# Moving a second attention into the segment loop of a tuned kernel, giving an output projection four column tiles of 128 outputs, and reordering the segment

## The chip, the cores and the metric

The kernel runs on one core of one Trainium2 chip. The metric is the device time of one execution, in microseconds (us). Before the change it was 1159.68 us, the median of three runs (1159.42 to 1160.88). TensorE is called PE below, ScalarE ACT, VectorE DVE, GpSimd POOL; PEld is PE's weight load, which runs beside the matmuls (in before PE is busy for 1012.0 us and PEld for 559.7, in a span of 1153.9).

## The reference, cut to what matters

Two attentions work on the same 2048 x 512 input, and a gate per token mixes their results.

```
# A: 64 segments of 32 tokens, 32 heads of 128, 8 memory tokens carried on
mem = mem0
for s in range(64):
    h = concat([mem, x[32*s : 32*s+32]])           # 40 tokens
    q, k, v = h @ Wq, h @ Wk, h @ Wv               # each 512 -> 32 heads x 128
    p = softmax(mask(q @ k^T * scale))
    o = einsum(p @ v, Wo)                          # 4096 -> 512
    mem, out[s] = o[:8], o[8:]                     # the next segment needs mem

# B: 4 blocks of 512 tokens, 32 heads of 16; block by block causal softmax attention
#    plus a linear memory M, z of the earlier blocks; then @ wo
result = g * A + (1 - g) * B                       # g: sigmoid gate per token
```

A is one long chain: segment s+1 cannot be projected before segment s has left Wo. B has no such chain and can fill gaps. The kernel cuts B into 160 **steps**: the scores and the exp of one step, then its product with V. Ten steps make one of 16 **jobs** (4 heads on each half of the partitions; the operands of a job are brought from DRAM, to which the projections of B were stored).

## The kernel before

A static order of units is emitted for every segment; each engine is given its instructions in that order, with semaphores where one engine needs another's result.

```
A_ORDER = """
    K1 K0 Q0 Q1 Fc TK0 TQ0 TK1 Ff bP TQ1 bT Fc S0 bS V0 M0 S1 N0 V1 M1 N1 PV0 Fc E0a E0b PV1 W0 E1a E1b W1 Fc bP bP bS
    WT bS Ff bT""".split()
```

K, Q, V are the projections of head groups 0 and 1; TK, TQ the transposes; S the scores with their exp (ACT); M the softmax sums with Ln and Exp on ACT; N the normalization (DVE); PV the product with V; E its evictions; W the two halves of Wo; WT the transposition of Wo's result into the next segment's input. bS, bP, bT are pieces of B. Fc and Ff are **fill units**: projections of the last 8 tokens of the four segments of a group, which are not on the chain (Fc), and their transposes and the end of a finished group (Ff).

Wo before, per segment: 32 matmuls of 512 columns. Each of four column tiles (32 token rows) holds a partial sum over 8 of the 32 heads; the partial sums are added afterwards by a product with a selector `selL`, for which the float32 result is split into a high and a low bfloat16 part.

```
for i in range(4):
    for j in range(4):                                   # column tile j: heads 16b+4j+i
        h = 16 * b + 4 * j + i
        ins = pe.matmul(pb[bk][SEG * j:SEG * (j + 1), :], OT_sb[:, h, 0:SEG], Wo_sb[:, h, :], ...)
...                                                      # after b == 1:
evac("act", aW_sb[:, 0, cs], pb[bk][:, cs], ...)                                       # hi, twice
P.op("dve", ... d.tensor_tensor(aW_sb[:, 1, cs], pb[bk][:, cs], aW_sb[:, 0, cs], ALU.subtract))  # lo, twice
...                                                      # w_t: 8 products with selL, adding hi and lo
ins = pe.matmul(pb[bk][:, SEG * c:SEG * (c + 1)], aW_sb[:, k, 128 * c:128 * (c + 1)], selL[:, :], ...)
```

Ahead of the loop stand B's projections, mixed with 40 of the 160 B steps. For those steps the job's buffers are double (`KTa`/`KTb`, `QTa`/`QTb` and so on); the other 120 steps run in the loop with one set of buffers. [... loads, constants, gates and the scheduler are cut ...]

## Time and profile before

| what | value |
|---|---|
| time, median of 3 | 1159.68 us |
| stage 1, up to the first segment | 0 to 174 us, granted clock 0.81 |
| segment loop, 64 segments | 174 to 1146 us, 15.2 us a segment, granted clock 1.00 |
| end | 8 us |

The first two lines below are from the profile's page of the kernel before; each digit stands for a fortieth of the span (29 us). "PE" is its busy share in tenths, "PEclk" the clock that PE was granted, in tenths of full speed (9 means 0.9 or more).

```profile
PE   4667769999999999999999999999999998988886
PEclk8798779999999999999999999999999998999999
```

The windows view of before gives the same by stages: length, busy time of each engine with its instruction count, the mean granted clock, the share in which DMA engines were busy, and GB/s.

```profile
core 0: us, PE busy (x) PEld busy (x) DVE busy (x) ACT busy (x) POOL busy (x), PEclk, DMA share, GB/s
0.00:174.00 174.00, 113.19 (x987) 57.68 (x1005) 57.49 (x111) 69.85 (x95) 86.26 (x178) 0.81 0.56 186
174.00:1146.00 972.00, 896.27 (x23349) 500.86 (x23356) 432.18 (x1116) 620.70 (x1329) 162.42 (x395) 1.00 0.06 16
```

PE is idle for a third of stage 1 (busy for 113.19 of 174 us), and its clock is low there (0.81). In the loop PE is busy for 896 of 972 us at full clock: it is the limit. The little that it waits is in the view of PE's waits of before (line and result that waited, releaser, us in total, times, longest):

```profile
PE ps L1102 <- DVE Pn_sb L1092: 25.4, 62, 0.9
PE ps L1160 <- ACT LN_sb L312: 14.8, 31, 0.9
PE ps L726 <- DMA QTa<-scr_qTd: 13.1, 5, 11.8
...
PE ps L1160 <- ACT VL L312: 4.8, 11, 0.9
PE ps L1160 <- DVE aW_sb L1149: 4.7, 4, 1.4
```

L1102 is PV, waiting for the normalized probabilities `Pn_sb`: 0.4 us in nearly every segment. L1160 is the product with the selector. It waits 24.3 us in the whole run (14.8 + 4.8 + 4.7), 0.4 us a segment. The timeline of PE in before (start, length, line, result and operands, count; in brackets the idle time just ahead and what ended it) shows the stretch from the first scores to the second PV:

```profile
560.33 1.05 PE L876 MATMUL ps<-Wv_sb,hT 128*32 128x512 bf16 x16
561.21 0.27 PE L1077 MATMUL ps<-P_sb,onesb 128*32 128x160 bf16 x8
...
561.40 0.27 PE L1050 MATMUL ps<-QT_sb,KT_sb 128*32 128x40 bf16 x16
561.50 0.29 PE L1054 MATMUL ps<-QT_sb,KTL 128*32 128x16 bf16 x16
561.62 1.06 PE L876 MATMUL ps<-Wv_sb,hT 128*32 128x512 bf16 x16
562.50 0.28 PE L1077 MATMUL ps<-P_sb,onesb 128*32 128x160 bf16 x8
562.72 0.27 PE L1102 MATMUL ps<-Pn_sb,V_sb 32*128 32x40 bf16 x16
...
563.01 0.62 PE L876 MATMUL ps<-Wq_sb,xL 128*32 128x512 bf16 x8
564.01 0.28 PE L1102 MATMUL ps<-Pn_sb,V_sb 32*128 32x40 bf16 x16 [0.39 <-DVE Pn_sb L1092]
```

Both V projections (0.87 us each, from start to start) and one fill unit (`Wq_sb,xL`) lie inside the stretch and cover nearly all of ACT's and DVE's chain. (The 16 score matmuls of 40 columns at 561.40 take 0.10 us to the next start, 6.5 ns each.) I call it the **thin stretch**, since this is where PE has least to do of its own.

### The profile page before, as it was taken

What the parts mean: (1) busy time and instruction counts of PE and PEld (TensorE: products, weight loads), DVE (VectorE), ACT (ScalarE), POOL (GpSimd) and SP (SyncE); (2) the same over time, 40 slices, a digit from 0 to 9 for tenths busy, and PEclk for the clock granted to TensorE, in tenths of its full rate; (3) what the DMA queues carried; (4) which work ended last, traced back from release to release, by engine and by line L of the source; (5) the groups of instructions that cost most, each with busy time, mean ns of one, the idle gap of its engine ahead of it and who ended that gap; (6) DMA issues with size and microseconds to landing.
All of it is one profiled execution on the core that took longest, in us unless ns stands there. A gap on an engine that the chain in (4) does not pass through costs nothing. (4 is left out here: it accounts for less than half of the span.)

```text
span 1153.9 us, 54295 instructions
## 1 busy us (share of the span) xinstructions
PE 1012.0 (88%) x24359; PEld 559.7 (49%) x24389; DVE 491.1 (43%) x1229; ACT 692.1 (60%) x1427; POOL 248.7 (22%) x573
## 2 busy tenths in 40 slices
PE   4667769999999999999999999999999998988886
PEld 2333325555555555555555555555555554544443
DVE  2333334444444444444444444444444443434333
ACT  2455336666666666666666666666666664555554
POOL 6554431211212121212122111212122110000000
PEclk8798779999999999999999999999999998999999
DMA  9486310010101001010100001010100000000000
GB/s 309 141 278 226 105 62 3 3 32 4 36 5 27 13 11 29 8 32 8 27 12 23 12 9 31 8 33 7 28 12 23 18 3 21 3 12 4 12 12 7
DMA packets 50943, 47.59 MB, mean 41 GB/s; under 512 B 23184, under 2 KB 49176, under 8 KB 49176
## 3 DMA queue, kind: packets, MB, share of 16 engines
q1 hardware_dynamic: 50712, 44.13, 12.3%
q8 instruction: 192, 3.15, 1.1%
q14 instruction: 39, 0.32, 0.1%
HBM read 31.50 MB, written 12.61 MB: 38 GB/s over the span
## 5 line engine op out<-in xcount | busy, mean ns | idle before, releaser
L742 POOL TENSOR_SCALAR_AFFINE_SELECT PTa<-PTa 128x256 bf16<-128x256 bf16 (+1 forms) x205 | 90.1, 440 | 419.1 <-ACT PTa L734 387.6
L734 ACT ACTIVATE PTa<-ps 128x1024 bf16<-128x1024 f32 x147 | 150.4, 1024 | 42.2 <-PE ps L726 40.6
L876 PE MATMUL ps<-Wv_sb,hT 128*32 128x512 bf16 x2048 | 134.9, 381 | 2.0 <-ACT QT_sb L312 1.3
L312 ACT ACTIVATE QN_sb<-ps 128x512 bf16<-128x512 f32 x128 | 76.4, 597 | 89.5 <-PE ps L876 89.5
L876 PE MATMUL ps<-Wk_sb,hT 128*32 128x512 bf16 x2048 | 123.3, 383 | 3.7 <-DVE hT L1166 2.6
L1139 PE MATMUL ps<-Wo_sb,OT_sb 128*32 128x512 bf16 x2048 | 126.2, 381 | 0.1
L876 PE MATMUL ps<-Wq_sb,hT 128*32 128x512 bf16 x2048 | 121.6, 379 | 0.0
L314 DVE CAST V_sb<-ps 128x512 bf16<-128x512 f32 x128 | 88.5, 691 | 73.1 <-PE ps L1077 40.5
L1149 DVE TENSOR_TENSOR aW_sb<-ps,aW_sb 128x256 bf16<-128x256 f32 x128 | 48.4, 420 | 128.1 <-ACT aW_sb L312 126.1
L312 ACT ACTIVATE aW_sb<-ps 128x256 bf16<-128x256 f32 x128 | 42.2, 381 | 92.5 <-PE ps L1139 92.5
L1191 POOL COPY OTL<-OT_sb 128x256 bf16<-128x256 bf16 x64 | 25.4, 397 | 319.4 <-DVE OT_sb L314 319.4
L312 ACT ACTIVATE OT_sb<-ps 128x320 bf16<-128x320 f32 x192 | 75.7, 428 | 24.9 <-PE ps L1111 24.9
L312 ACT ACTIVATE QT_sb<-ps 128x512 bf16<-128x512 bf16 x128 | 77.0, 601 | 22.3 <-PE ps L885 22.3
L876 PEld LDWEIGHTS ps<-Wq_sb,hT 128*32 128x32 bf16 x2048 | 54.8, 97 | 55.8
L726 PE MATMUL ps<-QTa,KTa 32*128 32x512 bf16 (+1 forms) x448 | 55.6, 305 | 24.4 <-DMA QTa<-scr_qTd 13.1
L314 DVE CAST KN_sb<-ps 128x512 bf16<-128x512 f32 x64 | 44.2, 690 | 75.6 <-PE ps L876 75.6
L876 PEld LDWEIGHTS ps<-Wk_sb,hT 128*32 128x32 bf16 x2048 | 49.2, 97 | 53.5 <-DVE hT L1166 5.1
L314 DVE COPY KT_sb<-ps 128x512 bf16<-128x512 bf16 x64 | 27.2, 425 | 111.0 <-PE ps L885 111.0
L1139 PEld LDWEIGHTS ps<-Wo_sb,OT_sb 128*32 128x32 bf16 x2048 | 46.6, 95 | 49.9 <-ACT OT_sb L312 20.7
L876 PEld LDWEIGHTS ps<-Wv_sb,hT 128*32 128x32 bf16 x2048 | 47.2, 95 | 38.1 <-issue 6.7
L312 ACT ACTIVATE KN_sb<-ps 128x512 bf16<-128x512 f32 x64 | 38.2, 597 | 43.2 <-PE ps L876 43.0
L1081 ACT ACTIVATE R_sb<-ps 128x160 f32<-128x160 f32 x128 | 38.8, 303 | 33.7 <-PE ps L1077 33.3
(146 smaller groups left out, 1802.5 us busy)
## 6 DMA issues: line engine op xcount, KB each, us to landing
Wk_sb<-in_A_Wk_dram SPq DMA_DIRECT2D x4, 1024.0 KB, 7.9
Wq_sb<-in_A_Wq_dram SPq DMA_DIRECT2D x4, 1024.0 KB, 5.6
Wv_sb<-in_A_Wv_dram SPq DMA_DIRECT2D x4, 1024.0 KB, 6.4
Wo_sb<-in_A_Wo_dram SPq DMA_DIRECT2D x4, 1024.0 KB, 6.3
scr_vd<-V SPq DMA_DIRECT2D x16, 136.0 KB, 2.2
Wo_sb<-in_A_x_dram SPq DMA_DIRECT2D x4, 512.0 KB, 8.2
scr_kTd<-stgk SPq DMA_DIRECT2D x16, 128.0 KB, 3.9
scr_qTd<-stgq SPq DMA_DIRECT2D x16, 128.0 KB, 4.6
```

Of the source, the lines that this page charges most:

```text
L312: P.op("act", lambda a: a.activation(dst, src, ACT.Copy), reads=[v.rbank[k] for k in bks], writes=dres, name=name)
L314: P.op("dve", lambda d: d.tensor_copy(dst, src), reads=[v.rbank[k] for k in bks], writes=dres, name=name)
L726: ins = pe.matmul(v.pb[bks[x]][:, o:o + w], KT[e][r, 128 * kc:128 * (kc + 1)], QT[r, q0:q0 + w], start=True, stop=True, tile_position=(r.s ...
L734: P.op("act", lambda a: a.activation(pt[:, :, :], v.ps[:, bks[0]:bks[1] + 1, :], ACT.Exp, scale=v.SCALE_B), reads=[v.rbank[b] for b in bks ...
L742: P.op("gp", lambda g, mv=mv: g.affine_select(mv, mv, [[0, mv.shape[1]], [1, 128]], ALU.is_ge, 0.0, base=0, channel_multiplier=-1), reads= ...
L876: ins = pe.matmul(pb[bk][SEG * j:SEG * (j + 1), :], lhs(c), w_sb[:, c, n0:n0 + 512], start=(c == 0), stop=(c == C - 1))
L1081: P.op("act", lambda a: a.activation(R_sb[:, b, :], pb[bk][:, 224:384], ACT.Ln), reads=[rbank[bk]], writes=[Rs("R%d" % b)], name="ln%d_%d" ...
L1139: ins = pe.matmul(pb[bk][SEG * j:SEG * (j + 1), :], OT_sb[:, h, 0:SEG], Wo_sb[:, h, :], start=(b == 0 and i == 0), stop=(b == 1 and i == 3))
L1149: P.op("dve", lambda d, cs=cs: d.tensor_tensor(aW_sb[:, 1, cs], pb[bk][:, cs], aW_sb[:, 0, cs], ALU.subtract), reads=[rbank[bk], Rs("aWh%d ...
L1191: P.op("gp", lambda gq: gq.tensor_copy(OTL[par][:, :, 8 * r:8 * r + 8], OT_sb[:, :, SEG:L]), reads=[Rs("OT%d_%d" % (c, hf)) for c in range ...
```

## The change

The intent has three parts. (1) No B step ahead of the loop any more: stage 1 holds only projections, and all 160 steps become fill in the loop; the results of A and B pass through DRAM, and the buffers of the B jobs become single. (2) Wo gets column tiles of 128 outputs each: 128 matmuls of 128 columns instead of 32 of 512. Each tile sums over all heads, so no partial sums, no split and no selector remain; one transpose makes the next input. (3) A new order of the segment. The diff, cut to its core (cuts marked by dots):

```diff
 A_ORDER = """
-    K1 K0 Q0 Q1 Fc TK0 TQ0 TK1 Ff bP TQ1 bT Fc S0 bS V0 M0 S1 N0 V1 M1 N1 PV0 Fc E0a E0b PV1 W0 E1a E1b W1 Fc bP bP bS
-    WT bS Ff bT""".split()
+    Q0 K0 K1 Q1 TK0 bP TQ0 TK1 TQ1 V0 S0 bS M0 Ff bT S1 N0 V1 M1 N1 PV0 E0b bP E0a PV1 E1a E1b bP bS Ff bT Fc Fc W0 W1
+    bS WT Ff""".split()
 ...
-                for i in range(4):
+                for h in range(16 * b, 16 * b + 16):
                     for j in range(4):
-                        h = 16 * b + 4 * j + i
-                        ins = pe.matmul(pb[bk][SEG * j:SEG * (j + 1), :], OT_sb[:, h, 0:SEG], Wo_sb[:, h, :],
-                                        start=(b == 0 and i == 0), stop=(b == 1 and i == 3))
+                        ins = pe.matmul(pb[bk][SEG * j:SEG * (j + 1), 0:128], OT_sb[:, h, 0:SEG], Wo_sb[:, h, 128 * j:128 * (j + 1)],
+                                        start=(h == 0), stop=(h == H - 1))
 ...
-                for k in range(2):
-                    evac("act", aW_sb[:, 0, cs], ...)          # hi
-                for k in range(2):
-                    P.op("dve", ... ALU.subtract ...)           # lo
+                evac("dve", aW_sb[:, :], pb[bk][:, 0:128], [bk], [Rs("aW")], "aW%d" % s)
 ...
-            for k2 in range(2): ... 8 products with selL ...
+            P.op("pe", lambda pe: pe.transpose(pb16[bk][:, 0:128], aW_sb[:, :], ident[:, :]), ...)
 ...
-    for n in range(n_pre):                                      # 40 B steps among the projections
-        bat.scores() ... bat.pv()
+    for n in range(len(pieces)): ... pieces[n]()                # projections alone
 ...
-    n_b0, nseg_b = bat.n, DEV.get("nseg_b", 51)
+    n_b0, nseg_b = bat.n, DEV.get("nseg_b", 57)
```

The fill units of projections also become whole (16 matmuls instead of two halves of 8), and four of the copies out of PSUM (where PE's results go, `ps` in the views; the kernel uses it in banks) change between ACT and DVE (`A_ENG`). In the new order V0 stands ahead of S0; no Fc stands between PV0 and PV1.

## The prediction

It was made from the code, the diff and the profile of before alone.

> **What bounds the kernel now.** The windows view shows three stages. (1) 0 to 174 us, until the first segment's K projection: projections of B mixed with 40 of the 160 B steps. PE is 64% busy and its mean granted clock 0.6 to 0.9 [...]. Waits between engines bound it. (2) 174 to 1146 us: 64 segments of 15.1 us, PE 93 to 95% busy at clock 1.00. From starts in the timeline I count 14.1 us of issued work and 0.8 us of idle a segment (0.37 before the second PV, on DVE Pn_sb; 0.25 before the selL product). (3) 8 us of end.
>
> **Removed.** Per segment the hi/lo split (ACT 2 x 381 ns, DVE 2 x 420 ns, in series) and 8 selL matmuls (0.46 us of PE). From the end of Wo to the next K takes 2.3 us with nothing between (last segment, timeline); a DVE copy of 128 columns (about 0.29 us, from casts of 490 and 690 ns for 320 and 512), a transpose and the hT cast (190 ns) should take 1.1. Stage 1 loses 40 B steps (about 0.7 us of PE, 1.02 of ACT each), their loads and chains.
>
> **Added, moved.** Wo becomes 128 matmuls of 128 columns: the same streaming, 4 times the instructions. The 40-column score matmuls issue every 6.5 ns, so issue is no limit: 1.8 to 2.0 us against 1.8. The loop gets 2.8 B steps a segment for 2.35: +0.3 us of PE. The new order puts V0 ahead of the scores and the fill behind E1. From the first scores to the second PV takes 4.4 us (timeline), set by ACT (exp, the 1.02 us B exp, Ln, Exp, exp, Ln, Exp). PE fills all but 0.4 us of it now; the new order leaves it about 2.9 us of work there. So I expect about 1 us of new idle, which eats the gain at the segment's end: 15.2 to 15.7 us with B steps, 14.2 in the last seven. All jobs now have single buffers, with scores slots 4 to 6 us apart, against 6.8 us from the first K load to Q's landing: waits of 1 to 3 us in about 10 of 16 job changes (now 1.3 us in most of the loop), some on V; 10 to 45 us in all.
>
> **Sum (estimates from those durations).** Stage 1: 65 us of PE, or 24 MB at the first slice's 300 GB/s, 80 us; with left projections and start-up 95 (-78). Loop: 57 x 15.4 + 7 x 14.2 + 25 of DMA waits = 1003 (+31). End: aT through DRAM, two groups in series: 18 (+9). Total 1116 us; range 1075 to 1148. Faster by over 2%: 0.70; within 2%: 0.27; slower: 0.03.
>
> **Signs.** Right: first segment near 95 us, higher clock before it; the aW split gone; PE idle before the sums and the second PV grows; PE waits on DMAs of QTj and Vj in the loop; PE busy under 93% in the loop; the last 18 us thin. Wrong: segments of 14.5 us or less without new idle (then about 1060), or Wo over 2.2 us.
>
> **What would make it wrong.** Stage 1 stalling on stores queued behind 1 MB weight loads; ACT's order misjudged; Wo's weight loads not hidden; clock drops from new idle.

## The result, and the profile after

The kernel after took 1241.14 us, the median of four runs (1229.38 to 1242.89), against 1159.55 us for before in the same rounds (1157.56 to 1160.88). The ratio is 1.068, with a 95% interval of 1.062 to 1.075: **slower by 6.8%**, where 1116 us and a gain had been predicted. Ratios here and below are the mean time of one kernel's fast runs over that of the other's of the same rounds, so they are not quite the ratios of the medians quoted.

The same two lines of the page, for after (a digit is 31 us):

```profile
PE   8978888888888898878898988798879888888884
PEclk9989999899989899889899989899999989999997
```

The windows of after, by its own stages:

```profile
0.00:90.00 90.00, 74.08 (x525) 37.14 (x529) 48.84 (x99) 36.73 (x63) 24.71 (x93) 0.94 0.87 289
90.00:1219.00 1129.00, 974.07 (x29512) 596.55 (x29503) 482.65 (x1207) 552.75 (x1112) 187.18 (x452) 0.94 0.08 23
1219.00:1240.00 21.00, 7.34 (x57) 2.97 (x56) 2.40 (x4) 2.25 (x4) 0.00 (x0) 0.65 0.16 44
```

Stage 1 did what was wanted: the loop starts at 90 us instead of 174. Nearly all the loss is in the loop: 1129 us instead of 972 (the end takes 21 instead of 8). PE is busy in 86% of it instead of 92%, and its granted clock is 0.94 instead of 1.00. PE's waits of after:

```profile
PE ps L1078 <- DVE Pn_sb L1068: 37.2, 59, 0.9
PE ps L704 <- DMA QTj<-scr_qTd: 28.0, 12, 3.2
PE ps L1053 <- ACT P_sb L1036: 19.9, 71, 0.6
PE ps L751 <- DMA MZj<-scr_mzd: 13.8, 7, 3.7
PE ps L855 <- ACT R_sb L1057: 13.0, 23, 0.8
PE ps L1124 <- DVE aW_sb L321: 9.5, 25, 0.6
...
PE ps L1114 <- issue: 4.3, 11, 0.9
```

Two families of waits are new or larger. Three of them (L1078, L1053, L855) are the thin stretch: PV, sums and the V1 projection waiting for the softmax chain. Two (L704, L751) are B steps waiting for the operands of the next job. (`P_sb` holds the exp of the scores, `R_sb` the reciprocals of their sums; `QTj`, `KTj` and `Vj` are a job's operands, `MZj` its part of the linear memory.) The timeline of PE in after shows in one segment what such waits do:

```profile
338.13 1.05 PE L855 MATMUL ps<-Wv_sb,hT 128*32 128x512 bf16 x16 [0.73 <-ACT R_sb L1057]
...
340.51 0.28 PE L1078 MATMUL ps<-Pn_sb,V_sb 32*128 32x40 bf16 x16 [0.64 <-DVE Pn_sb L1068]
...
343.46 0.36 PE L751 MATMUL ps<-Vj,PT 128*128 128x17 bf16 x8 [2.58 <-DMA MZj<-scr_mzd]
...
344.83 3.40 PE L855 MATMUL ps<-Wv_sb,xL 128*32 128x512 bf16 x32
348.06 1.95 PE L1114 MATMUL ps<-Wo_sb,OT_sb 128*32 128x128 bf16 x128
```

The 32 matmuls at 344.83 took 3.40 us. In the next segment, 32 matmuls of the same shape take 1.91 us. The trace's own record of the granted clock has one half for 6.83 us from 341.1 us on: right after the waits of 0.73 and 0.64 us, with only short matmuls between, and across the wait of 2.58 us. The last line is Wo in its new form, back at full clock: 1.95 us, or 1.89 from its start to the next one's, inside what had been predicted (1.8 to 2.0).

The clock record was counted for every kernel: in the loop of before there is **one** stretch at half clock (6.8 us), in after there are **29** (126 us). The records of before and after hold no other values than 1.0 and 0.5, and every stretch at 0.5 in their loops lasts 3.41 or 6.83 us (ahead of the loop of before also 13.65 and 17.07 us).

A least-squares fit over the 57 segments of after that hold B steps separates the terms: a segment takes 16.4 us, plus 0.43 us for each us at half clock (2.16 us in the mean), plus 0.79 us for each us of waiting for a B load (0.77 us in the mean). The same fit for before has 15.2 us as its first term. The 0.43 has a standard error of 0.04; the same fit has 0.48 for h2 (below), and over the other kernels it spreads from 0.3 to 0.8. A fit shows what goes together and is no experiment. So four quantities need a cause: a longer clean segment, the halved clock, the load waits, and whatever the new Wo does.

### The profile page after: what moved, and what is told of

Read it like the earlier page. It is cut to its first block, busy times and chain, and to the rows that moved or that the text cites. A ratio compares the mean times of both kernels' runs of the same rounds, so it can differ in the third digit from the quotient of the medians.

```text
span 1240.0 us, 65228 instructions
## 1 busy us (share of the span) xinstructions
PE 1055.5 (85%) x30085; PEld 636.7 (51%) x30085; DVE 533.9 (43%) x1309; ACT 591.7 (48%) x1179; POOL 211.9 (17%) x544
## 3 DMA queue, kind: packets, MB, share of 16 engines
q1 hardware_dynamic: 55320, 48.32, 12.8%
## 4 chain that ended last, share of the span: by engine, by line
PE 71%; ACT 8%; DMA 6%; DVE 6%; SPq 5%; issue 3%; ACTq 0%; POOL 0%; DVEq 0%
PE ps L855 34%; PE ps L1114 10%; PE ps L864 6%; SPq L664 5%; PE ps L918 3%; ACT PT L712 3%; DMA QTj<-scr_qTd 3%; PE ps L583 2%; PE ps L558 2%; PE ps L751 2%; PE ps L704 2%; ACT R_sb L1057 2%; ACT P_sb L1036 1%; ACT R_sb L1060 1%; DMA MZj<-scr_mzd 1%
## 5 line engine op out<-in xcount | busy, mean ns | idle before, releaser
L712 ACT ACTIVATE PT<-ps 128x1024 bf16<-128x1024 f32 x160 | 163.8, 1024 | 133.1 <-PE ps L704 128.5
L720 POOL TENSOR_SCALAR_AFFINE_SELECT PT<-PT 128x256 bf16<-128x256 bf16 (+1 forms) x224 | 98.4, 439 | 637.2 <-ACT PT L712 632.8
L855 PE MATMUL ps<-Wv_sb,hT 128*32 128x512 bf16 x2048 | 134.4, 381 | 16.1 <-ACT R_sb L1057 13.0
L321 DVE CAST KN_sb<-ps 128x512 bf16<-128x512 f32 x128 | 88.6, 692 | 124.7 <-PE ps L855 124.7
L1114 PEld LDWEIGHTS ps<-Wo_sb,OT_sb 128*32 128x32 bf16 x8192 | 128.4, 100 | 26.9 <-issue 15.1
L855 PE MATMUL ps<-Wq_sb,hT 128*32 128x512 bf16 x2048 | 135.1, 384 | 6.1 <-DVE hT L1128 4.3
L1114 PE MATMUL ps<-Wo_sb,OT_sb 128*32 128x128 bf16 x8192 | 136.1, 224 | 4.8 <-issue 4.3
L855 PE MATMUL ps<-Wk_sb,hT 128*32 128x512 bf16 x2048 | 123.7, 384 | 0.0
L704 PE MATMUL ps<-QTj,KTj 32*128 32x384 bf16 (+3 forms) x512 | 65.6, 313 | 28.1 <-DMA QTj<-scr_qTd 28.0
L855 PEld LDWEIGHTS ps<-Wk_sb,hT 128*32 128x32 bf16 x2048 | 55.6, 98 | 57.7 <-issue 3.5
L1064 DVE TENSOR_TENSOR Pn_sb<-P_sb,R_sb 128x160 bf16<-128x160 bf16 x128 | 46.0, 359 | 80.9 <-ACT R_sb L1060 77.6
L855 PEld LDWEIGHTS ps<-Wq_sb,hT 128*32 128x32 bf16 x2048 | 49.3, 97 | 55.8 <-DVE hT L1128 9.1
L751 PE MATMUL ps<-Vj,PT 128*128 128x17 bf16 x1280 | 57.4, 172 | 19.2 <-DMA MZj<-scr_mzd 13.8
L855 PEld LDWEIGHTS ps<-Wv_sb,hT 128*32 128x32 bf16 x2048 | 44.9, 95 | 51.8 <-ACT R_sb L1057 15.3
L1036 ACT ACTIVATE P_sb<-ps 128x224 bf16<-128x224 f32 x128 | 44.7, 350 | 52.6 <-PE ps L1030 51.4
L1078 PE MATMUL ps<-Pn_sb,V_sb 32*128 32x40 bf16 x2048 | 35.3, 178 | 39.2 <-DVE Pn_sb L1068 37.2
```

The costliest lines, as they stand in the source:

```text
L321: P.op("dve", lambda d: d.tensor_copy(dst, src), reads=[v.rbank[k] for k in bks], writes=dres, name=name)
L704: ins = pe.matmul(v.pb[bks[x]][:, o:o + w], KT[e][r, 128 * kc:128 * (kc + 1)], QT[r, q0:q0 + w], start=True, stop=True, tile_position=(r.s ...
L712: P.op("act", lambda a: a.activation(pt[:, :, :], v.ps[:, bks[0]:bks[1] + 1, :], ACT.Exp, scale=v.SCALE_B), reads=[v.rbank[b] for b in bks ...
L720: P.op("gp", lambda g, mv=mv: g.affine_select(mv, mv, [[0, mv.shape[1]], [1, 128]], ALU.is_ge, 0.0, base=0, channel_multiplier=-1), reads= ...
L751: ins = pe.matmul(v.pb[ob][:, o:o + 17], pt[:, x, col:col + 128], V[:, kc, 17 * h:17 * (h + 1)], start=first, stop=True, skip_group_check= ...
L855: ins = pe.matmul(pb[bk][SEG * j:SEG * (j + 1), :], lhs(c), w_sb[:, c, n0:n0 + 512], start=(c == 0), stop=(c == C - 1))
```

## The experiments

Five theories were tried against one another. The texts use their numbers.

- **Theory 1**: the new order takes PE work out of the thin stretch; the chain on ACT and DVE then shows as idle time, and idle time halves the clock.
- **Theory 2**: the new Wo, with four times the matmuls, costs time by itself.
- **Theory 3**: the single buffers of the B jobs make steps wait for loads.
- **Theory 4**, formed after the first runs: PE's instruction fetch runs dry where many short instructions follow one another, which is in the new Wo.
- **Theory 5**: moving the B steps into the loop costs more there than stage 1 gives back.

Sixteen kernels ran, all with results that match the reference. "Half clock" is the number and total of half-clock stretches in the loop. The ratio of each to before has its 95% interval in brackets.

### e1: the new Wo alone, all else as before

```diff
-                for i in range(4): ... 32 matmuls of 512 columns, hi/lo, 8 products with selL
+                for h in range(16 * b, 16 * b + 16): ... 128 matmuls of 128 columns, one copy, one transpose
```

> The kernel before with only the new Wo: 128 matmuls of 128 columns, one cast, one transpose, in the old order, with 40 B steps still ahead of the loop. Theory 1 (the order of units leaves TensorE idle between the scores and the second PV, and its clock is halved for it; Wo is innocent): 0.46 us of selL products and about 0.25 us of idle go from each segment, about 0.2 us comes back, so 1115 to 1140 us, no more than 2 half-clock stretches in the loop. Theory 2 (four times as many Wo instructions cost TensorE and disturb its issue): 1160 us or more.

Measured: 1238.32 us, 1.066 [1.062, 1.071]; half clock 13 stretches, 47.8 us. Theory 1 had this run faster than before. It is 77 us slower, so this change costs nearly the whole difference *by itself in the old order*. PE's waits of e1, and its timeline at one Wo:

```profile
PE ps L1138 <- issue: 61.0, 47, 2.2
PE ps L1102 <- DVE Pn_sb L1092: 24.3, 60, 0.9
```

```profile
584.89 1.54 PE L1138 MATMUL ps<-Wo_sb,OT_sb 128*32 128x128 bf16 x94
588.04 0.68 PE L1138 MATMUL ps<-Wo_sb,OT_sb 128*32 128x128 bf16 x34 [1.61 <-issue]
```

94 matmuls run, then PE stands still for 1.61 us with nothing in the profile that it waits for ("issue"), in the middle of a group of independent matmuls. The page lists one DMA queue that carries nothing but instructions; of before and of e1:

```profile
q8 instruction: 192, 3.15, 1.1%
```

```profile
q8 instruction: 236, 3.87, 1.3%
```

(packets, MB, share of the 16 engines). Each packet is 16,384 bytes in the traces of before and after. The new Wo has 128 weight loads and 128 matmuls where there were 64 instructions, and loses 14 at the selector: 178 more in each of 64 segments, 11,392 in all. The queue carries 44 packets more, so 259 instructions a packet, or about 64 bytes each (an estimate from these counts). By it one new Wo, 256 instructions, is about one whole packet, used up in 1.89 us where nothing stalls (from start to start in the segment of after shown above). Set against the times of these packets in the trace, the stalls of e1 line up:

```
stall ended (us)  idle (us)  at line  after the end of a packet (us)  after its start (us)
190.1             0.76       L1138    1.36                            2.47
207.6             1.56       L1138    1.34                            2.35
237.9             1.56       L1138    1.41                            2.37
269.5             1.58       L1138    1.22                            2.42
351.7             1.90       L1138    1.33                            2.36
```

All 43 stalls of over 0.3 us end 1.22 to 1.60 us after a packet has landed and 2.2 to 2.9 us after it has started, and all sit at the same place of the instruction stream, counted modulo 256 (within the few records that the trace misses). I read this as a boundary between two packets, and it made theory 4.

### f1: the new Wo in the old order, spread out

```diff
-    ... PV0 Fc E0a E0b PV1 W0 E1a E1b W1 Fc bP bP bS
+    ... PV0 Fc E0a E0b PV1 bP W0 E1a E1b Fc bP W1 bS
```

> The kernel before with the new Wo, as in the first run (1238 us, where the second half of Wo waited 61 us for nothing that the profile shows, and went on 1.2 to 1.6 us after a 16 KB instruction fetch had ended), but with B steps and a fill unit put between PV, W0 and W1, so that no 256 instructions follow each other in under 2.4 us. Theory 4 (TensorE runs out of instructions in the burst of 256 of Wo): the issue waits fall under 20 us, half-clock stretches in the loop from 13 to under 5, time 1125 to 1165 us. If these waits have another cause, they stay near 60 us and the time stays above 1210 us.

Measured: 1221.56 us, 1.055 [1.050, 1.059]; "issue" waits at Wo 53.1 us in 47 places, half clock 14 stretches. A miss, and by the text it even speaks against theory 4 (waits near 60 us, over 1210 us). One piece of B ahead of Wo, and a half fill unit with another piece between its halves, brought 17 us, and not the time down to the expected 1125 to 1165. But the kept trace shows the stalls of e1 again: the 44 "issue" stalls of over 0.3 us at Wo end 1.20 to 1.60 us after a packet has landed. So their ends still follow the packets; what failed is the idea of how much spacing helps. Spacing of this size left most of the stalls (53.1 us for 61.0).

### g3: the old Wo with 192 idle instructions added

96 one-column matmuls with a zero operand are put among the 32 of the old Wo in the kernel before; they add zero. Wo then has 256 instructions, as the new one, but the old data flow.

```diff
+                    for k in range(12):
+                        j = k % 4
+                        ins = pe.matmul(pb[bk][SEG * j:SEG * (j + 1), 0:1], OT_sb[:, h, 0:SEG], v.zed[:, :], start=False, ...)
```

> The kernel before, whole, with 96 matmuls of one column (times zero, into the same sums, so the output is the same) put between the 32 of Wo: Wo's instructions rise from 64 to 256 as in the change, its 512-column tiles, evacuation and order stay. Theory 4: issue waits of 30 us or more appear in Wo and right behind it, each ending 1.2 to 1.6 us after a 16 KB instruction fetch; with about 0.6 us of extra issue a segment 1220 to 1290 us. If the count of instructions is harmless: no issue waits, 1160 to 1205 us.

Measured: 1279.23 us, 1.103 [1.099, 1.107]. The "issue" waits appear, 30.7 us (30 times) at the added line and 11.8 us (10 times) at the old matmuls, where before has none among its 13 largest waits:

```profile
PE ps L1144 <- issue: 30.7, 30, 1.8
PE ps L1140 <- issue: 11.8, 10, 1.8
```

Those of over 0.3 us end 1.21 to 1.60 us after a packet has landed, as in e1. Half clock 15 stretches, 64.8 us. So the stalls come with the number of instructions and not with the new tiles or their data. The rest of the 118 us is not settled in its parts: the added matmuls take about 0.6 us a segment themselves (12 of them 0.08 us in the timeline), and the clock is halved for 58 us more.

### g5 and g1: the other two corners of order and Wo

g1 is part one of the change alone: B in the loop and results through DRAM as in after, with the old order, the old Wo and the old half fill units. g5 is g1 with the new Wo. e5 is after with the old Wo.

```diff
# g1, against after: old A_ORDER, old A_ENG, fill units in halves, old Wo
# g5, against g1: new Wo
# e5, against after: old Wo
```

> Part one of the change alone: all B steps in the loop, projections ahead, outputs through DRAM at leisure; but the Wo, the order of units, the half fill units and their kept banks of before. If moving the steps is sound (what costs is Wo's burst of instructions and the order made for it): stage 1 ends near 95 us, segments with B steps take 15.2 to 15.8 us where they do not wait for a load, half-clock stretches in the loop under 15, all of them at waits for loads, 1090 to 1150 us. If the steps in the loop cost more than they save (theory 5): 1160 us or more.

> The run before with the new Wo as its only difference. Theory 4 (instruction fetch): issue waits of 40 to 65 us in Wo, half-clock stretches up by about 10, 40 to 80 us slower than the run before. If Wo is innocent in this frame: 20 to 40 us faster than it.

> The changed kernel with the Wo of before put back (32 matmuls of 512 columns, hi and lo parts, selL products). Theory 1: the chain from Wo to the next segment gets longer by about 1.2 us with little work to cover it in the new order, so 1270 to 1330 us. Theory 2 (the new Wo costs): 1180 to 1225 us.

Measured:

| us, median (ratio to before) | old Wo | new Wo |
|---|---|---|
| old order | g1 1160.54 (0.999 [0.996, 1.002]) | g5 1243.23 (1.070 [1.066, 1.074]) |
| new order | e5 1313.46 (1.131 [1.126, 1.137]) | after 1241.14 (1.068 [1.062, 1.075]) |

The two parts are not additive. In the old order the new Wo costs 83 us; in the new order it saves 72. One line of PE's waits from g5, and one from e5, say why:

```profile
PE ps L1119 <- issue: 55.5, 42, 2.1
```

```profile
PE ps L1136 <- DVE aW_sb L1125: 68.7, 60, 1.4
```

In the old order (g5) Wo stands behind dense groups of short matmuls (PV) and the fetch runs dry, as in e1: 55.5 us of stalls, and half clock in 26 stretches (136.5 us, where g1 has 68.3). In the new order two whole fill units, 32 long matmuls in all, precede Wo (1.74 us for the 64 instructions ahead of Wo at 364.57 us), and the "issue" wait is 4.3 us in after. So the new order hides these stalls. That it is these two units is argued, not tested alone; it fits that with only one of them ahead of Wo the wait is 12.6 us (f2, below, against 4.3 in after) and 9.6 us (h4, against 3.7 in h2). But with the old Wo in it (e5), the split hi/lo has one B step left between W1 and WT, and shows as 68.7 us of waiting. The old order had hidden just this: 4.7 us in before, 4.8 in g1. The new order and the new Wo need one another, and together they come out where the new Wo comes out in the old order. g5 lost a little more on g1 than expected (83 us; 40 to 80). g1 came a little above its expected range (1090 to 1150): part one had gained nothing yet, with half clock in 12 stretches and this wait:

```profile
PE ps L704 <- DMA QTj<-scr_qTd: 26.1, 12, 5.1
```

### h1 and h2: the loads of the B jobs in halves

Theory 3 is tested without more memory: five of a job's ten steps use one half of its heads. So each half of the K, Q and V buffers is loaded for the next job as soon as the last step of that half is done.

```diff
-    def load(self, job, part):
+    def load(self, job, part, G=0):
+        q = slice(64 * G, 64 * (G + 1))                         # rows of the half
+        ld(v.QTj[q, :], v.qTd[sb, f, q, :], ...)
...
-        if n % 10 == 9:
-            self.load(job + 1, "k")
+        if k == 4:                                              # fifth step of the half
+            self.load(job + 1, "k", G)
```

h1 is g1 with this, h2 is after with this.

> Part one alone, with the loads of a B job in halves of 4 heads: the rows of K and Q and the columns of V of one half are loaded for the next job as soon as its last step is done, 5 steps ahead of their use, in the same memory. Theory 3: waits of the B scores and PV for loads fall under 6 us in all, half-clock stretches in the loop under 6, 1060 to 1110 us, faster than both kernels. If the waits are not what halves the clock: within 15 us of part one alone.

> The changed kernel with the half loads and nothing else. The waits for loads of B jobs fall from about 45 us to under 5 us. Theory 1: half-clock stretches in the loop fall only to 12 to 22, those that start in the thin stretch, and an undisturbed segment stays at 15.7 to 16.0 us: 1160 to 1195 us. If the load waits alone halve the clock: under 6 stretches and under 1150 us.

Measured: h1 1110.47 us, 0.956 [0.953, 0.959], half clock 4 stretches, 20.5 us. h2 1178.10 us, 1.013 [1.011, 1.015], half clock 16 stretches, 58 us. h1 lies 0.5 us above its expected range; h2 lies inside, but its clean segment takes 16.4 us and not 15.7 to 16.0. The largest waits of PE in h1, and in h2, no longer hold a load of a job's operands:

```profile
PE ps L1086 <- DVE Pn_sb L1076: 21.9, 55, 0.9
PE ps L972 <- DMA oTg<-scr_oTd: 13.0, 7, 4.0
```

```profile
PE ps L1081 <- DVE Pn_sb L1071: 39.7, 64, 0.9
```

Two things follow. First, the load waits cost 63 us in after and 50 us in part one, more than the 43.6 us of waiting that after shows (28.0 `QTj`, 13.8 `MZj`, 1.8 `Vj`). With the fit's terms, 43.6 x 0.79 = 34 us for the waits and (126 - 58) x 0.43 = 29 us for the half clock that went with them, 63 us together (an estimate from the fit of after, and it agrees). Second, theory 5 falls: part one is a gain of 4.4% once its loads are early enough. What is left of after's loss, from h1 to h2, is 68 us, and that is the new order with the new Wo, the whole fill units and the moved copies; these last two were not tested alone.

### e3: two buffers for the K tiles

```diff
-          ("KTj", [128, 512], BF16, 2), ...
+          ("KTj", [128, 512], BF16, 4), ...
-            self.load(job + 1, "k")
+            self.load(job + 1, "q")
+            self.load(job + 2, "k")
```

> The changed kernel with two buffers for the K tiles of the B jobs, loaded a job ahead, and Q loaded first (one phi buffer fewer to make room). Waits of the B scores for the Q load fall from 28 us to under 8 us; with some half-clock stretches saved 1200 to 1225 us. Theory 3 (single buffers are the main cost): under 1180 us.

Measured: 1207.20 us, 1.042 [1.037, 1.047], inside the expected range. The `QTj` wait is gone from the list, `MZj` stays (12.8 us), half clock 25 stretches, 105.8 us. An earlier and weaker form of what h2 shows.

### h6: the new order's thin stretch in the best old-order kernel

Theory 1 by itself: h1 with no change but two moves in the order, V0 ahead of S0 and the Fc out from between the PVs to a place behind E1. The work is the same.

```diff
-    ... bT Fc S0 bS V0 M0 S1 N0 V1 M1 N1 PV0 Fc E0a E0b PV1 W0 E1a E1b W1 Fc bP bP bS
+    ... bT Fc V0 S0 bS M0 S1 N0 V1 M1 N1 PV0 E0a E0b PV1 W0 E1a E1b Fc W1 Fc bP bP bS
```

> The run with part one and half loads (1110 us, 4 half-clock stretches in the loop), with only its order changed so that the stretch from the scores to the second PV is as thin as in the change: V0 ahead of the first scores, the half fill unit between the two PV moved behind them. Theory 1: 0.7 to 1.1 us of new idle a segment ahead of the sums and of the second PV, half-clock stretches in the loop 10 or more, 1160 to 1220 us. If the order is innocent: 1100 to 1125 us.

Measured: 1200.56 us, 1.031 [1.028, 1.034], so 90 us slower than h1 for moving two units. Half clock 15 stretches, 51.2 us (h1: 4, 20.5). PE's waits of h6:

```profile
PE ps L1086 <- DVE Pn_sb L1076: 58.9, 64, 0.9
PE ps L858 <- ACT R_sb L1065: 24.9, 43, 0.8
PE ps L1061 <- ACT P_sb L1044: 19.5, 71, 0.6
```

They are the three of after's thin stretch, and 58.9 us stands against 21.9 in h1. The timeline of PE in h6 shows each of them in one segment:

```profile
572.15 0.28 PE L1061 MATMUL ps<-P_sb,onesb 128*32 128x160 bf16 x8 [0.24 <-ACT P_sb L1044]
...
573.28 1.05 PE L858 MATMUL ps<-Wv_sb,hT 128*32 128x512 bf16 x16 [0.53 <-ACT R_sb L1065]
...
575.66 0.28 PE L1086 MATMUL ps<-Pn_sb,V_sb 32*128 32x40 bf16 x16 [0.94 <-DVE Pn_sb L1076]
```

That is 1.7 us of idle in a stretch where h1 has 0.4. Theory 1 stands, and this is its cleanest test. The same fit as above has 16.5 us as first term for h6 and 15.4 for h1. But the 90 us are not the price in after, whose stretch is less thin: the three waits make 103.3 us in h6 and 70.1 in after.

### e2, f2, h4: the two units moved back in the changed kernel

V0 behind the first bS and one Fc between the PVs again, in after (e2); the same with the fill units on two banks of PSUM kept for them (f2); the same in h2, with PSUM banks handed out in the order of their release (h4).

```diff
-    ... TQ1 V0 S0 bS M0 Ff bT S1 N0 V1 M1 N1 PV0 E0b bP ... Fc Fc W0 W1
+    ... TQ1 S0 bS V0 M0 Ff bT S1 N0 V1 M1 N1 PV0 Fc E0b bP ... Fc W0 W1
# f2 and h4 also:
-                    bk = B.take()
+                    bk = B.take(long=True)
```

> The changed kernel with two units moved in the order of a segment and nothing else: V0 from ahead of the first scores to behind the first B scores, and one of the two fill units from ahead of Wo to between the two PV. Theory 1: idle ahead of the sums and of the second PV falls from about 1.4 us to under 0.5 us a segment, half-clock stretches in the loop from 29 to under 8, time 1100 to 1160 us. Theory 2 (Wo) and theory 3 (waits for the loads of the single-buffered B jobs) leave it at 1210 us or more, with the stretches still there.

> The run with two units moved again, but the fill projections take their PSUM banks from the two that the kernel before kept for them, so the moved fill unit cannot hold up the second PV by its bank. Theory 1 (thin stretch and halved clock): waits of PV on casts of LN and VL are gone, half-clock stretches under 10, 1120 to 1180 us. If the order is innocent: 1230 us or more.

> The run before with the two units moved back (V0 behind the first B scores, one fill unit between the two PV), the fill projections on the kept banks, and banks given out in the order in which they came free. Theory 1: idle in the stretch under 0.5 us, half-clock stretches under 8 but for issue waits of Wo, 1100 to 1150 us. If the order is innocent: no faster than the run before.

Measured: e2 1303.85 us, 1.119 [1.111, 1.127] (its profiled run fell in the slow state); f2 1257.90 us, 1.085 [1.082, 1.088]; h4 1163.59 us, 1.001 [0.998, 1.003]. Three misses. In e2 PV waits for DVE evictions that have nothing to do with it, since PSUM banks are handed out at planning time and moved units took banks that were still being read: 17.6 us on the copy of `LN_sb` and 9.2 on `VL` (slow run, so only the kind of wait counts). In f2 the largest `Pn_sb` waits at PV were down to two of 2.8 us (37.2 in after) and the median clean segment to 15.6 us (16.3 in after), as theory 1 says, but two segments of 31 us had all projections on one bank, and 33.7 us went to `QTj`. In h4 the `Pn_sb` waits at PV are 4.2 and 2.8 us (39.7 in h2), but the line

```profile
PE ps L1080 <- DVE V_sb L320: 37.1, 37, 2.6
```

has taken its place, so that it gained 15 us on h2 and missed the expected 1100 to 1150. Filling the thin stretch does remove its waits; in these kernels the banks turned most of that into a new wait. How much could be had is left open.

### e4, f3: keeping PE busy with useless work

Six 128 x 512 matmuls a segment that nobody reads are put into the thin stretch of after, on any bank (e4), or on a kept bank and left out where none is free (f3).

```diff
-    ... S0 bS M0 ... V1 M1 N1 PV0 E0b bP E0a PV1 ...
+    ... S0 bS J1 M0 ... V1 J2 M1 N1 PV0 E0b bP J3 E0a PV1 ...
```

> The changed kernel with 6 useless matmuls of 128x512 a segment put where TensorE waits (one ahead of the first sums, two ahead of the second, three ahead of the second PV): 1.3 us of extra work a segment, output unchanged. Theory 1 with the clock as the larger part: half-clock stretches in the loop fall from 29 to under 12, an undisturbed segment stays at 15.6 to 16.2 us, and the time falls to 1165 to 1215 us although work was added. If idle alone is the cost, and not the clock, the time stays at 1240 us or rises; so with theories 2 and 3.

> The useless matmuls again, with those two banks (skipped where neither is free), so that they wait for no evacuation. If the halved clock is a cost of its own: half-clock stretches in the loop from 29 to under 12, issue of an undisturbed segment at most 0.3 us longer, time 1190 to 1225 us. If it costs nothing beside the idle: 1240 to 1275 us.

Measured: e4 1301.97 us, 1.124 [1.117, 1.130], half clock 10 stretches, 47.8 us; f3 1263.06 us, 1.090 [1.086, 1.093], half clock 18 stretches, 88.7 us. With more work there were fewer half-clock stretches, 29 to 10 and 18, but in e4 the useless matmuls waited 78.0 us for a bank, and in f3 they lengthened the clean segment. By the texts both times lie where the halved clock would cost nothing beside the idle (e4: 1240 us or more; f3: 1240 to 1275), but neither is a clean test, for these reasons and since the stretches did not fall under 12 in f3. So neither prices the halved clock by itself; that it costs about half of its duration rests on the fits alone (0.43 us for each us in after, 0.48 in h2).

### h5: the best version

h1 with the loads for the end of a group planned one segment earlier.

```diff
+        if not late:
+            late.extend(soon)
+            soon.clear()
-            late.extend(tail_units(tails))
+            soon.extend(tail_units(tails))
```

> Part one with half loads, the loads of a finished group's two halves planned one segment ahead of their use. Waits for oTg fall from 13 us to under 3 us, with the half-clock stretches that follow them: 1085 to 1103 us; output unchanged.

Measured: 1106.60 us, 0.952 [0.950, 0.954]; half clock 3 stretches, 13.7 us; the wait for `oTg` fell from 13.0 us (7 times) to 8.9 (2). It beats both kernels: by 4.8% the one before, and the one after by 135 us. It is a little above the expected 1085 to 1103. It holds part one of the change, without the new order and without the new Wo.

## Why the prediction was wrong

What was right, point by point:

- **Stage 1.** Predicted start of the loop 95 us, measured 90. The saving was put at 78 us and is 83. The clock there rose from 0.81 to 0.94.
- **The end.** Predicted 18 us, measured 21.
- **Wo as work.** Predicted 1.8 to 2.0 us, 1.89 from start to start in the segment shown and 2.02 in the mean of after's clean segments; the DVE copy of 128 columns was estimated at 0.29 us, and its mean is 292 ns.
- **All named signs came**: idle ahead of the sums and of the second PV, waits of PE for DMA in the loop, PE below 93% busy in it (no test, since before had 92% there). The waits were the foreseen ones, though on `QTj` and `MZj`, hardly on `Vj` (1.8 us).

What was wrong is the loop: "57 x 15.4 + 7 x 14.2 + 25 of DMA waits = 1003". It took 1129. The 126 us come apart so (estimates from the fit):

| term of the sum | predicted | measured | difference |
|---|---|---|---|
| clean segment with B steps, 57 | 15.4 us | 16.4 us | 57 x 1.0 = 59 us |
| halved clock | no term | 57 x 2.16 us x 0.43 | 53 us |
| waits for B loads | 25 us | 57 x 0.77 us x 0.79 = 35 us | 10 us |
| last seven segments | 14.2 us | 14.8 us | 4 us |

1. **The step that failed first: "eats the gain at the segment's end: 15.2 to 15.7 us".** There was almost no gain there to eat. The prediction took the 2.3 us from Wo to the next K, to become 1.1, from the last segment, where no fill stands between. In the other segments the selector product waited 0.4 us in the mean (24.3 us in the whole run): all but that of the split was hidden behind bP, bP and bS, and off the critical path. Counted over the clean segments (no half clock, no wait for a DMA) of the kept traces, Wo and the selector took 1.78 + 0.42 us of PE's time in before, and Wo and its transpose take 2.02 + 0.11 in after; the wait behind Wo went from 0.33 to 0.18 us. That is a gain of 0.2 us a segment, where about 1.2 had been taken off. g5 and g1 show that in the old order the new Wo had nothing to give and much to lose. The new idle, put at about 1 us, was right in kind and rather too large: the three waits of the thin stretch make 1.1 us in the mean clean segment (0.24, 0.73 and 0.64 us are single ones), against 0.4 there in before. So a clean segment of after is 1.2 us longer than one of before: 0.7 us of idle (1.65 for 0.91 in all) and 0.5 us of work, nearly all of it B steps (scores and product with V 1.88 for 1.40; the prediction had +0.3).
2. **The sum had no term for the clock.** "clock drops from new idle" stands in the prediction's last paragraph as a possibility and was costed at nothing. The clock was halved in 29 places, put down here to the idle of the thin stretch, alone or with a load wait. That idle stands in every segment and the clock was halved in some only; what decides between them is not shown. A long gap was not needed: in h2 no wait for a B load is left, PE idles 1.6 us a segment in the mean, no gap of the loop is longer than 1.5 us, and the clock was still halved 16 times. h6 makes these stretches from the order alone (15 against 4), and h2 takes 13 of 29 away by removing the load waits.
3. **The load waits were a right mechanism with a small size**: 43.6 us of waits instead of 25, and 63 us in all with the clock that goes with them (after against h2).
4. **"The 40-column score matmuls issue every 6.5 ns, so issue is no limit" is right for 16 or 32 of them and wrong for 128.** The rate itself is in the trace of before (16 of them in 0.10 us). But the 256 instructions of a new Wo stood still for up to 2.2 us at a time, 61.0 us in all (e1), and the stalls of over 0.3 us ended 1.22 to 1.60 us after a packet of instructions had landed. In after, the new order hid it: 4.3 us. So this step cost little in the kernel as it stands; it explains why the new Wo could not simply be put into the old order.

So theory 1 (h6: 90 us), theory 3 (h2: 63 us) and theory 4 (e1, g5, g3) are shown; theory 2 is refuted in its plain form, since Wo and its transpose take PE 2.13 us for 2.20 of Wo and the selector before; theory 5 is refuted by h1. Left open are the price of the halved clock by itself, what decides when the next packet of instructions comes (f1's spacing failed), the parts of the whole fill units and of the moved copies, and what after would reach with the thin stretch filled and no bank conflicts (h4).

## What to carry to other kernels

Before a serial piece of work is credited as a gain, look at what it is hidden behind in the steady state, not in the last iteration where nothing hides it. When work is taken out of a stretch that PE has to itself, cost the idle and also the clock, which was halved for 3.41 or 6.83 us at a time in the loops of before and after: with 0.4 us of idle in that stretch the loop had 1 (before) and 4 such places (h1), with 1.1 us 16 (h2), with 1.6 us 15 (h6). Splitting each matmul of Wo into four shorter ones changed PE's own time little (2.02 us for 1.78) but needed four times the instructions; try long matmuls ahead of such a burst (here 4.3 us of stalls for 55.5, with the order as a whole; the long matmuls were not tested alone), and load the operands of a next job half by half as the last ones are used up rather than paying for a second buffer.
